# Fused attention, soft-MoE and squared-ReLU FFN on one core: the second layer's first pass cut into a quarter and a half of the inner dimension, with two weight slots moved behind w2

## The chip, the cores and the metric

The kernel runs on one NeuronCore of a Trainium2 chip. The metric is the device time of one execution in microseconds (us). The core has a matrix engine (PE, with its weight loads listed apart as PEld), a vector engine (DVE), a scalar engine (ACT), a general engine (POOL), and a queue engine (SP) that issues every DMA of this kernel, in program order.

## The reference, cut to what matters

Three layers follow one another. The last two concern us here.

```python
# attention in chunks of 32 rows, 4 x 8 heads, gives x: 3072 x 512
logits = x @ phi                              # 3072 x 32
slot_input = softmax(logits, axis=0).T @ x    # 32 x 512
for e in range(8):                            # 4 slots per expert
    slot_out[e] = relu(slot_input[e] @ w1[e]) @ w2[e]    # 512 -> 1024 -> 512
x = softmax(logits, axis=1) @ slot_out        # c @ slot_out, 3072 x 512
h = x @ w_in                                  # 512 -> 2048
g = s * relu(h) ** 2 + b
out = g @ w_out                               # 2048 -> 512
```

w1 and w2 are 16 MB each and are read once. w_in and w_out come as float64, 8 MB each, and are read as pairs of 32-bit words; the kernel turns each 1 MB piece into float32 with shifts, masks and multiplications.

## The kernel before, in words

**First part.** Attention and the sums over tokens run until about 126 us. Meanwhile SP loads w1 into sixteen slots of SBUF, 1 MB each.

**Slot stage.** `emit_w1` (8 steps) and `emit_w2` (16 steps) compute slot_out, 32 rows at a time, with weights as the moving operand. The slots of w1 are refilled with w2 as they come free, by `load_w`, which issues the next entries of the list `order`. Before the change `order` holds two pieces of w_in (numbers 2 and 3, the list `EARLY`) ahead of the last four pieces of w2. Between the steps of `emit_w2` PE transposes the gate c into `cpack` (`pack_c`), and at steps 11 and 12 it does two bursts of four matmuls whose product nobody reads (`warm(4)`, the fillers).

**Second layer.** h is not computed from x: since x = c @ slot_out, the kernel forms M = slot_out @ w_in (32 rows, kept in `mpack`) and then h = c @ M. The inner dimension of 2048 is cut into 16 columns of 128, called f, and into four groups of four f, called fb. M is made one fb at a time: `m_part` for fb 0, and `emit_m` and `emit_m2` for fb 1 to 3, at the items listed in `M_AT`.

**Items.** The work of the second layer is a list of 112 items, each one block of tokens and one f. Four blocks of 384 tokens (A: two, B: two) go in pairs, and three blocks of 512 tokens (C) go singly. For item n PE makes h (`emit_h`); ACT does relu, square and the rounded high part `ghi`; DVE makes the low part `glo`; and PE, three items later (`LA`), adds three products per 128 tokens into PSUM: ghi and glo with the high part `w_hi` of w_out (`emit_o`), ghi with the low part `w_lo` (`emit_o2`). At the end of a block's run the sums leave PSUM: whole ones go to the output, half ones wait in `part`. With `HF` = 8 the runs are: A over f 0 to 7, B over all 16, C over all 16, A over f 8 to 15.

**Conversions.** The table `cq` says at which item k a piece of w_in ("i", fb, j) or w_out ("o", f) is converted: one ACT operation (`cv_act`, line 579), three DVE operations (lines 589, 591, 598), and for w_out one more on ACT (line 813) and two more on DVE (lines 806, 808). Before the change they come every second item, from item 0 to 46. The w_in pieces of fb 0 and of fb 1 are converted in the slot stage instead (`early`, eight `tasks`). The 1 MB pieces pass through three slots in turn (`NRG`); `load_w` fills one when the conversion that read it last is done.

**What sets the order.** Each engine takes its instructions in the order in which the code emits them: `for n in range(LA + 1, ...)` at the end is the loop over items. There is no planner.

Of the kernel before, what the change touches and what calls it, by code (L numbers as in the profile page):

```python
# [26 lines left out]
SLOT = 2048  # L27
# [7 lines left out]
def kernel(  # L35
# [81 lines left out]
    with tc.manual_schedule():  # L117
# [45 lines left out]
        NRG, E_AT = 3, 4  # L163
        EARLY = [("wi", 2), ("wi", 3)]
# [26 lines left out]
        def load_w(n, cap=None):  # L191
            for _ in range(n):
                i = wnext[0]
                if i < (len(order) if cap is None else cap):
                    src = srcs[order[i][0]][order[i][1]]
                    p = at_[order[i]] if i < npre else (16 + (i - npre) % NRG) * SLOT
# [385 lines left out]
        def cv_dve(key, j):  # L582
            h, lf, a, w = cv[key]
            hi, ai = h.bitcast(I32), a.bitcast(I32)
            if key[0] == "i" and key[1] > 1:
# [104 lines left out]
        tasks = [("i", j // 4, j % 4) for j in range(8)]  # L690

        def early(k, part):
            key = tasks[k]
            if part == 0:
                cv_act(key, 0 if k < 4 else k % 2, wi_src(*key[1:]))
                cv_dve(key, 0)
            else:
                cv_dve(key, 2)
                cv_low(key, cv[key][1].rearrange("p (k f) -> p k f", k=2))
                wi_add(key)  # L700

        for i in range(9):
            if i < 8:
                emit_w1(i)
                if i >= 1:
                    load_w(2, npre - E_AT - len(EARLY))
                if i == 0:
# [59 lines left out]
        wide_r, wide_r2 = at512(18 * SLOT, 2), at512(18 * SLOT + 1024, 2)  # L767
# [5 lines left out]
        HF = NF // 2  # L773
# [3 lines left out]
        runs = [[(x, 0, HF) for x in A], [(x, 0, NF) for x in B]]  # L777
        runs += [[(x, 0, NF)] for x in C] + [[(x, HF, NF)] for x in A]
# [6 lines left out]
        part = [tiles("part", 3, DM), [area(19 * SLOT + DM * t, DM) for t in range(NTU)]]  # L785
        h_t, o_t = {}, {}

        def stage_a(k):
            key = cq.get(k)
            if key:  # L790
                if key[0] == "i":
                    w = wi_src(key[1], key[2])
                else:
                    w = wt[raw_of[key]].rearrange("p (f d t) -> p f d t", f=2, t=2)[:, key[1] % 2]
                cv_act(key, k // 2 % 2, w)
# [19 lines left out]
        def emit_m(fb):  # L815
            wis = wis_b if fb % 2 else wis_a
            mp = psum("s", [128, 512])
            for lo in range(1 if fb == 1 else 2):
                for kc in range(KD):
                    lhsT, rhs = (soTb[:, kc, :], wis_l[:, kc, :]) if lo else (soT4[:, kc, 0, :], wis[kc // 2][:, kc % 2, :])  # L820
                    nc.tensor.matmul(out=mp[32 * kc:32 * kc + 32, :], lhsT=lhsT, rhs=rhs,
                                     start=(lo == 0), stop=(lo == 1 or fb == 1))
# [24 lines left out]
        def emit_hs(n):  # L847
            if n < len(items):
                if wide(n) or n // 2 - 1 in (M_AT[1] // 2, M_AT[2] // 2):
# [35 lines left out]
        wsum_hl = [cpack[:, 128 * B[0][0] + DM * x:128 * B[0][0] + DM * (x + 1)] for x in range(2)]  # L885
# [15 lines left out]
        def os_early(j, t):  # L901
            return area(16 * SLOT + DM * (NTU * j + t), DM)

        def add_bias(i):
            j, t = divmod(i, NTU)
            os_ = os_early(j, t) if j < 2 else part[j - 2][t]
            nc.gpsimd.tensor_tensor(out=os_, in0=os_, in1=bias, op=ALU.add)  # L907
            if j < 2:
                store(B[j][0] + t, os_)
# [17 lines left out]
        def emit_o2(n):  # L927
# [3 lines left out]
            for t in range(nt):  # L931
# [5 lines left out]
                if f == f1 - 1:  # L937
                    if r_[0] in B or f1 == HF:
                        to = os_early(B.index(r_[0]), t) if r_[0] in B else part[A.index(r_[0])][t]
                        if t == 1:  # L940
                            nc.scalar.activation(out=to, in_=o, func=AF.Copy, scale=sbt[:, 0:1])
                        else:
                            nc.vector.tensor_scalar(out=to, in0=o, scalar1=sbt[:, 0:1], scalar2=None, op0=ALU.mult)
                    else:
                        os_ = os_g[t]
                        nc.vector.scalar_tensor_tensor(out=os_, in0=o, scalar=sbt[:, 0:1],
                                                       in1=part[A.index(r_[0])][t] if f0 else bias,
# [75 lines left out]
        for n in range(LA + 1, len(items) + LA + 1):  # L1023
# [7 lines left out]
            if n == 2 * HF + 3:  # L1031
# [20 lines left out]
            if n != 2 * HF + 2:  # L1052
                convert(n)
            if 48 <= n < 64:
# [8 lines left out]
            while n != 2 * HF + 2 and wnext[0] < len(order) and last_use.get(order[wnext[0] - NRG], -1) <= n:  # L1063
# [73 lines left out]
```

## Time and profile before

| | us |
|---|---|
| median of 3 runs (lowest, highest) | 470.21 (468.28, 471.7) |
| profiled execution, its own time | 470.53 |
| its span, first to last instruction | 468.7 |
| PE busy in the span | 448.5 (96%) |
| ACT, DVE, POOL busy | 298.0, 285.5, 85.2 |
| mean granted clock of PE | 0.999 of full speed |

The time outside the span is 1.8 us. All 40 slices of the span show the granted clock at 9 tenths or more. The mean DMA rate is about 400 GB/s until 164 us, and then falls, because the weights are in. How to read it: a row of the timeline gives start and duration, then engine, line, operation and tiles; in brackets stands how long the engine had been idle and what ended that. Durations of neighbouring matmuls overlap, so the step from one start to the next is the cost of one, not the duration.

### The profile page before, as it was taken

Reading aid. Unit: us, or ns where it says so; the run is one execution under the profiler, and the core shown is the slowest. Engines: PE = TensorE matmul, PEld = TensorE weight load, DVE = VectorE, ACT = ScalarE, POOL = GpSimd, SP = SyncE. Lnnn points to the kernel's source line nnn. Section 1 sums busy time; section 2 is a strip of 40 time slices with the busy share of each in tenths; the row PEclk is TensorE's granted clock in tenths of the full one; section 3 lists DMA queues with packets and bytes.
Section 4 is the critical chain, followed back from the end, with each engine's and each line's share of the span. In section 5 each row is a group of like instructions: output and inputs, shape, how many; then the busy total and the mean of one; then the engine's idle time right before and its main releaser. Section 6 shows DMA issues by size and latency. Waiting matters only on the chain.

```text
span 468.7 us, 10048 instructions
## 1 busy us (share of the span) xinstructions
PE 448.5 (96%) x3936; PEld 339.6 (72%) x3936; DVE 285.5 (61%) x637; ACT 298.0 (64%) x588; POOL 85.2 (18%) x154
## 2 busy tenths in 40 slices
PE   6879999999899989999999999999999999999996
PEld 5656666666545556888786887888888888888885
DVE  5768888877466659978284988765642242224242
ACT  4556666657234559978686988666666666665670
POOL 6655556562000000000000000000690000000000
PEclk9999999999999999999999999999999999999999
DMA  8999999998999963424232000000320020002011
GB/s 298 357 398 385 404 407 405 405 403 324 402 418 421 415 280 96 175 89 162 89 109 90 0 2 0 1 0 1 123 103 1 0 89 2 0 2 87 2 69 67
DMA packets 20575, 83.03 MB, mean 177 GB/s; under 512 B 2736, under 2 KB 2864, under 8 KB 14640
## 3 DMA queue, kind: packets, MB, share of 16 engines
q1 hardware_dynamic: 20528, 82.39, 45.5%
q8 instruction: 31, 0.51, 0.4%
q14 instruction: 16, 0.13, 0.1%
HBM read 76.09 MB, written 6.29 MB: 176 GB/s over the span
## 4 chain that ended last, share of the span: by engine, by line
PE 71%; DMA 15%; DVE 6%; ACT 4%; issue 1%; SPq 1%; POOL 1%; DVEq 0%; POOLq 0%; ACTq 0%
PE g L924 12%; DMA vals<-in_vm_dram 6%; PE lp L924 6%; PE pt L924 6%; PE xt L924 6%; PE x L924 6%; PE g L936 6%; PE s L843 4%; DMA keys<-in_w_out_dram 4%; DMA seg<-in_w_dram 3%; PE s L285 3%; PE xt L936 3%; PE pt L936 3%; PE lp L936 3%; PE x L936 3%; PE x L325 3%
## 5 line engine op out<-in xcount | busy, mean ns | idle before, releaser
L878 DVE TENSOR_TENSOR glo<-vals,ghi 128x512 fp32r<-128x512 f32 x48 | 35.9, 752 | 63.2 <-ACT ghi L874 63.2
L866 ACT ACTIVATE vals<-s 128x512 f32<-128x512 f32 x48 | 28.7, 597 | 45.3 <-PE s L843 45.3
L878 DVE TENSOR_TENSOR glo<-r,ghi 128x384 fp32r<-128x384 f32 x64 | 35.4, 555 | 19.7 <-ACT ghi L874 19.5
L866 ACT ACTIVATE r<-s 128x384 f32<-128x384 f32 x64 | 31.2, 487 | 16.6 <-PE s L843 16.6
L301 ACT ACTIVATE seg<-seg 128x384 f32<-128x384 f32 x32 | 28.8, 899 | 19.8 <-DVE seg L312 15.6
L907 POOL TENSOR_TENSOR keys<-keys,bias 128x512 f32<-128x512 f32 x6 | 8.8, 1493 | 173.4 <-ACT vals L866 173.4
L936 PE MATMUL g<-wlo,ghi 128*128 128x512 f32 x128 | 39.6, 389 | 0.0
L924 PE MATMUL g<-whi,ghi 128*128 128x512 f32 x126 | 39.3, 390 | 0.0
L924 PE MATMUL g<-whi,glo 128*128 128x512 f32 x126 | 39.1, 389 | 0.0
L843 PE MATMUL s<-cpack,mpack 128*128 128x384 f32 (+1 forms) x112 | 36.9, 368 | 0.5 <-ACT r L866 0.4
L870 ACT ACTIVATE r<-r 128x384 f32<-128x384 f32 x64 | 33.6, 526 | 4.7 <-DVE glo L878 2.8
L263 POOL TENSOR_SCALAR keys<-keys 64x416 f32<-64x416 f32 x63 | 33.7, 534 | 13.9 <-PE lp L346 3.1
L285 PE MATMUL s<-keys 128*32 128x128 f32 x768 | 30.3, 291 | 4.6 <-POOL keys L267 3.3
L874 ACT CAST ghi<-r 128x384 fp32r<-128x384 f32 x64 | 32.6, 509 | 1.7 <-PE g L936 0.4
L325 PE MATMUL x<-vals,seg 128*32 128x128 f32 x744 | 27.8, 275 | 5.3 <-DMA vals<-in_vm_dram 4.4
L870 ACT ACTIVATE vals<-vals 128x512 f32<-128x512 f32 x48 | 30.4, 634 | 1.8 <-DVE glo L878 0.2
L325 PEld LDWEIGHTS x<-vals,seg 128*32 128x32 f32 x744 | 20.5, 109 | 15.0 <-DVE seg L309 5.2
L874 ACT CAST ghi<-vals 128x512 fp32r<-128x512 f32 x48 | 29.8, 621 | 1.5
L936 PEld LDWEIGHTS g<-wlo,ghi 128*128 128x128 f32 x128 | 24.0, 188 | 5.0
L924 PEld LDWEIGHTS g<-whi,glo 128*128 128x128 f32 x126 | 23.7, 188 | 5.1
L285 PEld LDWEIGHTS s<-keys 128*32 128x32 f32 x768 | 19.5, 113 | 10.6 <-POOL keys L267 6.0
L924 PEld LDWEIGHTS g<-whi,ghi 128*128 128x128 f32 x126 | 23.7, 188 | 4.5 <-issue 0.2
(257 smaller groups left out, 1052.3 us busy)
## 6 DMA issues: line engine op xcount, KB each, us to landing
seg<-in_w_dram SPq DMA_DIRECT2D x27, 1024.0 KB, 8.8
keys<-in_kq_dram SPq DMA_DIRECT2D x32, 396.0 KB, 7.4
vals<-in_vm_dram SPq DMA_DIRECT2D x64, 192.0 KB, 6.7
keys<-in_w_in_dram SPq DMA_DIRECT2D x5, 1024.0 KB, 5.0
keys<-in_w_out_dram SPq DMA_DIRECT2D x5, 1024.0 KB, 4.8
out_dram<-seg SPq DMA_DIRECT2D x18, 256.0 KB, 2.1
vals<-in_w_in_dram SPq DMA_DIRECT2D x3, 1024.0 KB, 8.6
vals<-in_w_out_dram SPq DMA_DIRECT2D x3, 1024.0 KB, 4.8
```

The lines of the kernel that those rows point to most:

```text
L263: (nc.vector if h and u == 0 else nc.gpsimd).tensor_scalar(out=stream(kz[rows, h], 0, CH), in0=k[rows, UT * h:UT * h + (NCU + 1) * CH].rea ...
L285: nc.tensor.matmul(out=o, lhsT=qt[:, 32 * c:32 * c + 32], rhs=kz[:, :, at:at + WIN], start=True, stop=not (first or last))
L301: nc.scalar.activation(out=p_r[u], in_=sm_r[u].rearrange("p t h (a r) -> p t r (h a)", a=2), func=AF.Exp, scale=scale)
L325: nc.tensor.matmul(out=xp[32 * r:32 * r + 32, t], lhsT=pts_r[u][:, 32 * c:32 * c + 32], rhs=vbuf[u // 2 % 2][:, u % 2, :, 64 * c:64 * c + ...
L843: nc.tensor.matmul(out=hq, lhsT=mpack[:, 128 * f:128 * f + 128], rhs=cpack[:, 128 * t0:128 * (t0 + nt)], start=True, stop=True)
L866: nc.scalar.activation(out=r_of(n), in_=h_t.pop(n), func=AF.Relu)
L870: nc.scalar.activation(out=r2_of(n), in_=r_of(n), func=AF.Square)
L874: nc.scalar.copy(out=g_of(n)[0], in_=r2_of(n))
L878: nc.vector.tensor_tensor(out=glo, in0=r2_of(n), in1=ghi.bitcast(F32), op=ALU.subtract)
L907: nc.gpsimd.tensor_tensor(out=os_, in0=os_, in1=bias, op=ALU.add)
L924: nc.tensor.matmul(out=o_t[r_][t], lhsT=g[x][:, 128 * t:128 * t + 128], rhs=w_hi[f], start=(first and x == 0), stop=False)
L936: nc.tensor.matmul(out=o, lhsT=ghi[:, 128 * t:128 * t + 128], rhs=w_lo[f], start=False, stop=(f == f1 - 1))
```

## The change

The items are cut differently: A runs over f 0 to 3 (`HA`), then B over f 0 to 7 (`HB`), then A over f 4 to 15, then C, then B over f 8 to 15. There are again 112 items. The order of the conversions changes with it: w_out f 0 to 3 at items 0, 2, 4, 6; w_in fb 1 at 7, 8, 9, 11; w_out f 4 to 7 at 13, 15, 17, 19; w_in fb 2 at 21 to 24 and fb 3 at 27 to 30; the rest of w_out as before. `early` keeps the four pieces of fb 0 only. The two pieces of w_in of fb 1 leave their place ahead of w2's last four pieces; they are loaded after w_out 0 and 1. The pieces pass through two slots instead of three. The sum for fb 1 moves from item 4 to item 12, and has a low part now, as those for fb 2 and 3 have. The fillers in the slot stage are gone. w2's last piece comes in three DMAs instead of two. Partial sums wait in other places, and half sums are added to in one more place on DVE and twice on POOL (`add_part`).

```diff
-        NRG, E_AT = 3, 4
-        EARLY = [("wi", 2), ("wi", 3)]
         order = [("w1", i) for i in range(W1)] + [("wi", 0), ("wi", 1)] + [("w2", i) for i in range(W2)]
...
-        order = order[0:-E_AT] + EARLY + order[-E_AT:]
-        order[W1:W1 + 3] = [("w2", 0), ("wi", 0), ("wi", 1)]
         npre = len(order)
-        at_.update({key: (18 + i) * SLOT for i, key in enumerate(EARLY)})
-        cq = {}
-        for j in range(8):
-            cq[2 * j] = ("o", j)
-            cq[16 + 2 * j] = ("i", 2 + j // 4, j % 4)
-            cq[32 + 2 * j] = ("o", 8 + j)
+        cq = {32 + 2 * j: ("o", 8 + j) for j in range(8)}
+        cq.update({k: ("o", j) for j, k in enumerate((0, 2, 4, 6, 13, 15, 17, 19))})
+        for fb, ks in enumerate(((7, 8, 9, 11), (21, 22, 23, 24), (27, 28, 29, 30))):
+            cq.update({k: ("i", fb + 1, j) for j, k in enumerate(ks)})
+        cbuf = {k: n % 2 for n, k in enumerate(sorted(cq))}
...
+        for n in range(npre, len(order)):
+            at_[order[n]] = (18 if n == npre + 2 else 16 + (n - npre - (n > npre + 2)) % 2) * SLOT
+        gate = {order[n]: max((last_use[key] for key in order[npre:n] if at_[key] == at_[order[n]]), default=-1)
+                for n in range(npre, len(order))}
...
-                        for x in range(2):
-                            nc.sync.dma_start(out=wt[order[i]][x], in_=src[:, SLOT // 2 * x:SLOT // 2 * (x + 1)])
+                        for x, w in ((0, 2), (2, 1), (3, 1)):
+                            at = slice(SLOT // 4 * x, SLOT // 4 * (x + w))
+                            nc.sync.dma_start(out=t[:, at], in_=src[:, at])
...
-        tasks = [("i", j // 4, j % 4) for j in range(8)]
+        tasks = [("i", 0, j) for j in range(4)]
...
                 if i >= 1:
-                    load_w(2, npre - E_AT - len(EARLY))
+                    load_w(2, npre)
...
-            if i == 2:
-                load_w(len(EARLY) + E_AT)
-            if i == 10:
-                load_w(2)
-            if i == 14:
-                load_w(1)
-            if i in (11, 12):
-                warm(4)
+            if i == 0:
+                load_w(3)
...
-            if 7 <= i < 15:
-                early(4 + (i - 7) // 2, (i - 7) % 2)
...
-        M_AT = (4, 26, 34)
+        M_AT = (12, 26, 34)
...
-        HF = NF // 2
+        HA, HB = NF // 4, NF // 2
...
-        runs = [[(x, 0, HF) for x in A], [(x, 0, NF) for x in B]]
-        runs += [[(x, 0, NF)] for x in C] + [[(x, HF, NF)] for x in A]
+        runs = [[(x, 0, HA) for x in A], [(x, 0, HB) for x in B], [(x, HA, NF) for x in A]]
+        runs += [[(x, 0, NF)] for x in C] + [[(x, HB, NF)] for x in B]
+        TURN = (2 * HA, 2 * HA + 2 * HB)
...
-            for lo in range(1 if fb == 1 else 2):
+            for lo in range(2):
...
+        def add_part(j):
+            nc.gpsimd.tensor_tensor(out=os_early(j, 1), in0=os_early(j, 1), in1=part[j][1], op=ALU.add)
...
+                        elif f1 < NF:
+                            nc.vector.tensor_scalar(out=to, in0=o, scalar1=sbt[:, 0:1], scalar2=None, op0=ALU.mult)
                         else:
-                            nc.vector.tensor_scalar(out=to, in0=o, scalar1=sbt[:, 0:1], scalar2=None, op0=ALU.mult)
+                            nc.vector.scalar_tensor_tensor(out=to, in0=o, scalar=sbt[:, 0:1], in1=part[x][t],
+                                                           op0=ALU.mult, op1=ALU.add)
...
-            late = m + 1 < len(items) and m + 1 == 2 * HF + 1
+            late = m in TURN
...
-            if n != 2 * HF + 2:
+            if n - 2 not in TURN:
                 convert(n)
+            if n in (53, 55):
+                add_part((n - 53) // 2)
...
-            while n != 2 * HF + 2 and wnext[0] < len(order) and last_use.get(order[wnext[0] - NRG], -1) <= n:
+            while n - 2 not in TURN and wnext[0] < len(order) and gate[order[wnext[0]]] <= n:
                 load_w(1)
```

On the SP queue, at the end of the slot stage's loads (`w_dram` is w1 or w2, `seg` 93 to 96 the slots of w2's last four pieces):

```order
-L212 DMA vals_103<-in_w_in_dram 128x2048
-L212 DMA vals_104<-in_w_in_dram 128x2048
 L212 DMA seg_93<-in_w_dram 128x2048
 L212 DMA seg_94<-in_w_dram 128x2048
 L212 DMA seg_95<-in_w_dram 128x2048
-L207 DMA seg_96<-in_w_dram 128x1024 x2
+L207 DMA seg_96<-in_w_dram 128x1024
+L207 DMA seg_96<-in_w_dram 128x512 x2
 L212 DMA keys<-in_w_out_dram 128x2048 x2
```

Two loads of 1 MB no longer stand ahead of w2's last four pieces and of w_out's first two.

On ACT, from the square of item 3 to the square of item 5, before the change (`ghi` is the high part of g, `whi` that of w_out, `mps` and `mpack` belong to the sum of M for fb 1):

```order
L870 ACTIVATE r_2650<-r_2648 128x384
L874 CAST ghi_2654<-r_2650 128x384
L579 ACTIVATE seg_99<-keys 128x512
L823 COPY mps_2646<-s 128x512
L866 ACTIVATE r_2647<-s 128x384
L870 ACTIVATE r_2649<-r_2647 128x384
L874 CAST ghi_2655<-r_2649 128x384
L813 CAST whi_2616<-seg_99 128x512
L832 CAST mpack<-s 128x512
L866 ACTIVATE r_2648<-s 128x384
L870 ACTIVATE r_2650<-r_2648 128x384
```

The same stretch after it:

```order
L864 ACTIVATE r_2619<-r_2617 128x384
L868 CAST ghi_2623<-r_2619 128x384
L579 ACTIVATE seg_99<-keys 128x512
L860 ACTIVATE r_2616<-s 128x384
L864 ACTIVATE r_2618<-r_2616 128x384
L868 CAST ghi_2624<-r_2618 128x384
L807 CAST whi_2585<-seg_99 128x512
L860 ACTIVATE r_2617<-s 128x384
L864 ACTIVATE r_2619<-r_2617 128x384
```

The copy `mps` and the cast into `mpack` have left this place; they stand at items 12 and 13 now.

On DVE, from item 9 to item 11 of the changed kernel, where the first run of A ends (line 941 takes sums out of PSUM into `part`; line 598 ends the conversion of a w_in piece into `seg_101`):

```order
L591 TENSOR_SCALAR seg_99<-vals_103 128x512
L598 SCALAR_TENSOR_TENSOR seg_101<-keys,seg_99 128x2x256
L941 TENSOR_SCALAR vals_103<-pt,cstt 128x512
L941 TENSOR_SCALAR vals_103<-xt,cstt 128x512
L872 TENSOR_TENSOR glo_2629<-r_2619,ghi_2624 128x384
L941 TENSOR_SCALAR vals_103<-lp,cstt 128x512
L941 TENSOR_SCALAR vals_104<-g,cstt 128x512
L589 TENSOR_SCALAR vals_104<-keys 128x2x256
L872 TENSOR_TENSOR glo_2625<-r_2618,ghi_2620 128x384
L591 TENSOR_SCALAR keys<-vals_104 128x512
L598 SCALAR_TENSOR_TENSOR seg_101<-keys 128x2x256
```

The last row here ends the conversion that the moved sum of M for fb 1 reads; four sums out of PSUM stand between it and the conversion before.

## Rows read from the trace of the kernel before

**Rows 1.** The windows view: busy time (instructions) by engine, clock, DMA share, GB/s.

```profile
159.50:166.90 7.40, 7.40 (x90) 4.17 (x86) 5.41 (x10) 1.91 (x5) 0.00 (x0) 1.00 1.01 415
166.90:171.90 5.00, 3.05 (x21) 2.05 (x17) 1.74 (x6) 2.98 (x8) 0.00 (x0) 1.00 0.93 382
171.90:186.40 14.50, 13.93 (x60) 9.64 (x61) 13.38 (x27) 14.08 (x30) 0.00 (x0) 1.00 0.22 84
186.40:208.00 21.60, 21.60 (x98) 18.08 (x98) 19.26 (x37) 20.05 (x42) 0.00 (x0) 1.00 0.43 148
```

**Rows 2.** The chain of waits: start us, us, what ended last.

```profile
135.48 15.73 DMA seg<-in_w_dram
...
151.28 18.33 DMA keys<-in_w_out_dram
```

**Rows 3.** Timeline of PE, 159 to 187 us: start us, us, operation, [idle before].

```profile
159.49 0.61 PE L449 MATMUL lp<-ident 128*128 128x256 bf16 x4
160.03 1.07 PE L666 MATMUL xt<-seg,seg 128*32 128x256 f32 x16
...
161.31 0.60 PE L449 MATMUL lp<-ident 128*128 128x256 bf16 x4
161.84 1.07 PE L666 MATMUL xt<-seg,seg 128*32 128x256 f32 x16
...
169.63 0.62 PE L843 MATMUL s<-cpack,mpack 128*128 128x384 f32 x2
...
186.14 0.44 PE L843 MATMUL s<-cpack,mpack 128*128 128x384 f32 x1 [0.40 <-ACT r L866]
```

**Rows 4.** Timeline of ACT, 168 to 188 us.

```profile
168.99 0.27 ACT L832 CAST mpack<-pt 128x128 fp32r<-128x128 f32 x1 [0.80 <-PE pt L686]
169.70 0.66 ACT L579 ACTIVATE seg<-keys 128x512 f32<-128x512 f32 x1 [0.45 <-DMA keys<-in_w_out_dram]
170.27 0.48 ACT L866 ACTIVATE r<-s 128x384 f32<-128x384 f32 x1
...
178.52 0.59 ACT L823 COPY mps<-s 128x512 f32<-128x512 f32 x1
179.00 0.50 ACT L866 ACTIVATE r<-s 128x384 f32<-128x384 f32 x1
...
180.51 0.62 ACT L813 CAST whi<-seg 128x512 fp32r<-128x512 f32 x1
181.10 0.59 ACT L832 CAST mpack<-s 128x512 fp32r<-128x512 f32 x1
181.58 0.50 ACT L866 ACTIVATE r<-s 128x384 f32<-128x384 f32 x1
...
185.60 0.49 ACT L866 ACTIVATE r<-s 128x384 f32<-128x384 f32 x1
...
187.52 0.48 ACT L866 ACTIVATE r<-s 128x384 f32<-128x384 f32 x1
```

**Rows 5.** Timeline of PE, h matmuls around the sum of M at 228 us.

```profile
217.19 0.51 PE L843 MATMUL s<-cpack,mpack 128*128 128x384 f32 x2
...
226.08 0.51 PE L843 MATMUL s<-cpack,mpack 128*128 128x384 f32 x2
...
237.31 0.51 PE L843 MATMUL s<-cpack,mpack 128*128 128x384 f32 x2
```

**Rows 6.** Timeline of DVE at the turn between two runs.

```profile
211.80 0.74 DVE L943 TENSOR_SCALAR vals<-g,cstt 128x512 f32<-128x512 f32 x1
212.46 0.42 DVE L591 TENSOR_SCALAR keys<-seg 128x512 int32<-128x512 int32 x1
212.91 0.69 DVE L598 SCALAR_TENSOR_TENSOR seg<-keys 128x512 bf16<-128x512 uint32 x1
213.51 0.55 DVE L878 TENSOR_TENSOR glo<-r,ghi 128x384 fp32r<-128x384 f32 x1
```

**Rows 7.** Page, section 6: a DMA issue, KB, us from issue to landing.

```profile
keys<-in_w_in_dram SPq DMA_DIRECT2D x5, 1024.0 KB, 5.0
```

More of the change, by code (lines that the diff above doesn't have):

```diff
@@ L195, in load_w @@
                     src = srcs[order[i][0]][order[i][1]]
-                    p = at_[order[i]] if i < npre else (16 + (i - npre) % NRG) * SLOT
+                    p = at_[order[i]]
                     if p is SPLIT:
@@ L584, in cv_dve @@
             hi, ai = h.bitcast(I32), a.bitcast(I32)
-            if key[0] == "i" and key[1] > 1:
+            if key[0] == "i" and key[1] > 0:
                 ai = wi_dst(wis_b if key[1] % 2 else wis_a, key).bitcast(I32)
@@ L694, in early @@
             if part == 0:
-                cv_act(key, 0 if k < 4 else k % 2, wi_src(*key[1:]))
+                cv_act(key, 0, wi_src(*key[1:]))
                 cv_dve(key, 0)
@@ L765, in at512 @@
             return [area(pos + 512 * i, 512) for i in range(n)]
-        wide_r, wide_r2 = at512(18 * SLOT, 2), at512(18 * SLOT + 1024, 2)
+        wide_r, wide_r2 = at512(17 * SLOT, 2), at512(17 * SLOT + 1024, 2)
         os_g = at512(13 * SLOT, 4)
@@ L784 @@
             items += [(r_, f) for f in range(rs[0][1], rs[0][2]) for r_ in rs]
-        part = [tiles("part", 3, DM), [area(19 * SLOT + DM * t, DM) for t in range(NTU)]]
+        part = [at512(18 * SLOT, 3), [area(18 * SLOT + 3 * DM, DM), bias, area(19 * SLOT + 3 * DM, DM)]]
+        part += [tiles("part", 3, DM), at512(19 * SLOT, 3)]
         h_t, o_t = {}, {}
@@ L794, in stage_a @@
                     w = wt[raw_of[key]].rearrange("p (f d t) -> p f d t", f=2, t=2)[:, key[1] % 2]
-                cv_act(key, k // 2 % 2, w)
+                cv_act(key, cbuf[k], w)
         def stage_d(k, j):
@@ L821, in emit_m @@
                     nc.tensor.matmul(out=mp[32 * kc:32 * kc + 32, :], lhsT=lhsT, rhs=rhs,
-                                     start=(lo == 0), stop=(lo == 1 or fb == 1))
+                                     start=(lo == 0), stop=(lo == 1))
             nc.scalar.copy(out=mps, in_=mp)
@@ L848, in emit_hs @@
             if n < len(items):
-                if wide(n) or n // 2 - 1 in (M_AT[1] // 2, M_AT[2] // 2):
+                if wide(n) or n // 2 - 1 in [x // 2 for x in M_AT]:
                     emit_h(n)
@@ L883, in wsum_add @@
                 nc.vector.tensor_tensor(out=wsum, in0=a, in1=(w_hi, w_lo)[i % 2][i // 2].bitcast(F32), op=ALU.add)
-        wsum_hl = [cpack[:, 128 * B[0][0] + DM * x:128 * B[0][0] + DM * (x + 1)] for x in range(2)]
+        wsum_hl = [cpack[:, 128 * t:128 * t + DM] for t in (A[0][0], C[0][0])]
         def wsum_split():
@@ L901, in os_early @@
         def os_early(j, t):
-            return area(16 * SLOT + DM * (NTU * j + t), DM)
+            return area(16 * SLOT + DM * j, DM) if t == 1 else part[j][t]
+        def add_part(j):
+            nc.gpsimd.tensor_tensor(out=os_early(j, 1), in0=os_early(j, 1), in1=part[j][1], op=ALU.add)
         def add_bias(i):
             j, t = divmod(i, NTU)
-            os_ = os_early(j, t) if j < 2 else part[j - 2][t]
+            os_ = os_early(j, t) if j < 2 else part[j][t]
             nc.gpsimd.tensor_tensor(out=os_, in0=os_, in1=bias, op=ALU.add)
             if j < 2:
-                store(B[j][0] + t, os_)
+                store(A[j][0] + t, os_)
         def emit_o(n, parts=(0, 1)):
@@ L937, in emit_o2 @@
                 if f == f1 - 1:
-                    if r_[0] in B or f1 == HF:
-                        to = os_early(B.index(r_[0]), t) if r_[0] in B else part[A.index(r_[0])][t]
+                    x = (A + B).index(r_[0]) if r_[0] in A + B else None
+                    if f1 < NF or x in (0, 1):
+                        to = part[x][t] if f1 < NF else os_early(x, t)
                         if t == 1:
                             nc.scalar.activation(out=to, in_=o, func=AF.Copy, scale=sbt[:, 0:1])
-                        else:
-                            nc.vector.tensor_scalar(out=to, in0=o, scalar1=sbt[:, 0:1], scalar2=None, op0=ALU.mult)
+                        elif f1 < NF:
+                            nc.vector.tensor_scalar(out=to, in0=o, scalar1=sbt[:, 0:1], scalar2=None, op0=ALU.mult)
+                        else:
+                            nc.vector.scalar_tensor_tensor(out=to, in0=o, scalar=sbt[:, 0:1], in1=part[x][t],
+                                                           op0=ALU.mult, op1=ALU.add)
                     else:
@@ L946, in emit_o2 @@
                         nc.vector.scalar_tensor_tensor(out=os_, in0=o, scalar=sbt[:, 0:1],
-                                                       in1=part[A.index(r_[0])][t] if f0 else bias,
+                                                       in1=bias if x is None else part[x][t],
                                                        op0=ALU.mult, op1=ALU.add)
@@ L1027 @@
             ends = 0 <= m and items[m][1] == items[m][0][2] - 1
-            late = m + 1 < len(items) and m + 1 == 2 * HF + 1
+            late = m in TURN
             if ends or late:
                 emit_o2(m)
-            if n == 2 * HF + 3:
+            if n - 3 in TURN:
                 convert(n - 1)
```

## The prediction, made before the changed kernel was run

> **What bounds the kernel now.** Read the windows view first, for the stretch that the change touches. At the end of the slot stage, 159.5 to 166.9 us, PE is busy 7.40 of 7.40 us while the DMA share is 1.01 at 415 GB/s [rows 1]: both are full, so one must ask which of them the other would wait for. PE's own rows answer: its steps follow one another without a bracket, and the fillers stand among them [rows 3]. So PE does not wait for w2 there. The transfers end only just in time: the chain of waits goes through two DMAs, the second of them w_out's first piece, which is issued at 151.28 and lands at 169.6 [rows 2], and ACT's first conversion had idled 0.45 us for it [rows 4]. From 166.9 to 171.9 PE is busy 3.05 of 5.00 us [rows 1]; there it follows copies and casts. From 186.4 to 208 it is busy 21.60 of 21.60 [rows 1], and no view shows it idle again until the tail. From about 186 us on, then, whatever PE must do more is paid in full, and only what shortens PE's work or moves its start is gained.
>
> The stretch between, 171.9 to 186.4, decides the sign. PE's busy time is 13.93 of 14.50 us, which reads as full. But it holds 60 matmuls, one in 0.242 us, where the next window has 98 in 21.60, one in 0.220; and PEld is busy 9.64 of 14.50 us (66%) against 18.08 of 21.60 (84%) [rows 1]. At its end the ninth h matmul waits 0.40 us for ACT's relu of item 7 [rows 3]. So this stretch, the ramp, goes at ACT's pace. The Trainium skill, page Trainium Kernel Development and Optimization, section Best Practices, says that matmul busy time is a bad measure of TensorE because matmuls are pipelined, and that the share of LDWEIGHTS is a better one. By that rule the ramp is not full, which the two shares above bear out; by busy time it is full, and the sum would be that of the first rival.
>
> **The change part by part.**
>
> *Fillers.* Two bursts of four matmuls cost PE 160.03 - 159.49 = 0.54 and 161.84 - 161.31 = 0.53 us [rows 3]. They lie on PE's path, which nothing interrupts: -1.07 us. The cover that could be missing is w2's data; it comes earlier now, as the next step says.
>
> *Two loads behind w2.* 2 x 1.05 MB at 415 GB/s [rows 1] are 5.0 us. So w2's last pieces and w_out 0 land 5 us earlier. PE gets none of that for w2, since it did not wait. What it gets is the 0.45 us at w_out 0: ACT was free at 168.99 + 0.27 = 169.26, and could start the conversion then and not at 169.70 [rows 4]. The relu behind it needs the first h matmul, though, one of a pair that runs from 169.63 to 170.25 [rows 3]; I estimate its product at 170.0. So relu moves from 170.27 to about 170.0: -0.25. Together with the fillers the second layer starts 1.3 us earlier. w_in 2 and 3 now land behind w_out; they are not needed before items 7 and 9, some 12 us after the layer starts, against 5.0 us for one such load [rows 7]: nothing.
>
> *The ramp on ACT.* The sum for fb 1 leaves it: the copy `mps` from 178.52 to the relu at 179.00, 0.48 us, and the cast into `mpack` from 181.10 to the relu at 181.58, 0.48 us [rows 4]. The conversion of w_in at item 7 is new in it. An item with one such conversion and no `whi` takes 187.52 - 185.60 = 1.92 us from relu to relu; without it, the way from relu at 179.00 to the end of `ghi` at 180.51 is 1.51 [rows 4]; so +0.41. By item 7's relu ACT is ahead by 1.3 + 0.48 + 0.48 - 0.41 = 1.85 us; I take 1.8, because DVE's steps between gain only the 1.3. The ninth h matmul, which waits for it, comes at 184.3 and not at 186.14 [rows 3]. From there PE is full, as before.
>
> *The sum of M for fb 1.* Before, its PE work lay in the ramp, where PE had room, and so cost nothing. Now it stands at item 12, behind the ramp, and has a low part like the others. Its price there is that of the sum for fb 2 at 228 us: four items without a sum go from the h pair at 217.19 to that at 226.08, 8.89 us; the next four, with it, to 237.31, 11.23 us [rows 5]. The difference, 2.34 us, is paid in full: +2.3.
>
> *The first turn.* A's run ends at item 7 now, among dense conversions. DVE steps there cost 0.66 us for a sum out of PSUM (211.80 to 212.46), 0.45 for line 591, 0.60 for line 598 and 0.47 for `glo` [rows 6]; with 0.4 for line 589 a conversion of w_in is 1.45. For items 7 to 11 that makes 4 x 1.45 + 4 x 0.66 + 5 x 0.47 + 1.4 for the rest of w_out 3, in all 12.2 us, against five items of PE at 8.89 / 4 = 2.22 us, or 11.1. DVE falls about 1.1 us behind. The moved sum needs the last conversion of these, at item 11, one item later. PE uses `glo` about two items after it is made, which hides most of it. Ends: nothing (the old turn, in the window to 208 us and beyond, shows no idle of PE) and 2.6 us (all four sums out of PSUM in PE's way). I take +0.4, near the end that a row shows.
>
> *The rest, at nothing.* The second turn, at item 24, has the same six sums as the old one, and conversions before and behind it rather than in it; if they collided it would be the first turn's 0.4 again. Two slots instead of three: a piece is asked for after the last use of its slot and is needed four to five items later, 8.9 us or more at PE's pace, against 5.0 us to land [rows 7]; for the tightest, w_in 5, ACT runs ahead by an item or two, and PE would feel it only when ACT's lead is gone. The two adds on POOL and the third DMA of w2's last piece are issued by queues that nothing waits for there. h matmuls and products are as many as before.
>
> **The sum.** -1.8 (which holds the 1.07 and the 0.25) + 2.34 + 0.4 = +0.94 us. The profiled execution took 470.53 us, 0.3 above the median of 470.21, and would take 471.5; from the median it is 471.2, which I forecast: no change that can be measured.
>
> **The rivals.**
>
> *The ramp is PE's, as its busy time says.* Then moving the sum of M is moving PE work within PE's path, and costs only its new low part: four matmuls side by side in the array's columns, by estimate the time of one product, 0.23 us (2.22 us hold nine and an h). The start's 1.3 us are kept. 470.21 - 1.3 + 0.23 + 0.4 gives 469.5. For it: 13.93 of 14.50. Against it: 0.242 us per matmul, and ACT's relu as the last releaser. 20%.
>
> *The slot stage goes at the DMA's pace.* If the fillers only filled waits, the second layer starts as much earlier as w_out 0 lands: -5.0 and not -1.3. Then 470.21 - 5.0 + 2.34 + 0.4 = 467.9. For it: the DMA share of 1.01, and w_out 0 in the chain. Against it: the products of the slot stage stand at even steps of PE, with and without a filler between. 7%.
>
> *DVE chokes at the first turn.* The place is between items 9 and 12. If the sums out of PSUM wait behind whole conversions, PE waits for its banks, and then for the conversion of item 11, without which M for fb 1 and so h for f 4 cannot come. It decides from the point where line 598 of item 11 ends later than PE's products of item 12. Price: the 2.6 us above in place of the 0.4: 473.4, slower than before; with a collision at the second turn too, 475.6. For it: 12.2 us of work in 11.1. Against it: two items' lead. 15%, a quarter of it with both turns.
>
> *PE's clock falls.* The granted clock is 1.00 in all four windows, also where PE idles 1.95 of 5.00 us [rows 1]; this is the higher of its levels, 2.4 GHz. The Trainium skill, page TensorE: Matmul & The Clock Gate, section The HAM clock gate, says that a PE left idle drops to half its clock, which speaks against taking fillers out. If it happened, the slot stage's end would take its 7.4 us of PE work again: 470.21 + 0.94 + 7.4 = 478.6. The trace disagrees so far as it goes, since the longer idle stretch keeps 1.00, and the change leaves no new gap. 2%.
>
> That the loads do not move is excluded by the order of the SP queue.
>
> **The numbers.** 56% for the forecast, with a range of its own from 470.0 to 472.5. With 20, 7, 15 and 2% for the others, the range that leaves out no more than two in ten goes from 468.4 (the sum of M free, -1.8) to 474.1 (-1.07 for the fillers alone, 2.34 and 2.6). The bound of what a measurement of this kernel can tell is 1%, 4.7 us. Faster than 465.5 needs more than the second rival gives: 3%. Slower than 474.9 takes both turns or the clock: 6%. Within: 91%.
>
> **What would show it.** In the changed profile the fillers' rows are gone and PE still has no bracket from 144 to 166 us; ACT's first conversion has no wait for a DMA; the first product with w_out 0 starts at about 170.6; the ninth h matmul at about 184.3; a step of 11.2 us and not 8.9 over the four items around item 12; no PE idle of more than 0.5 us at the first turn. I am wrong if the ninth h matmul comes before 183 (the first rival), if the slot stage ends before 164.5 (the second), or if PE waits for DVE at line 941 or 598 (the third).

## The result, and the profile after

| | before | changed |
|---|---|---|
| median of 15 runs each (lowest, highest), us | 469.39 (468.19, 471.7) | 472.79 (470.56, 473.79) |
| ratio to before, 95% interval | | 1.007 [1.0056, 1.0084] |
| profiled execution: its time, span, mean granted clock | 470.53, 468.7, 0.999 | 473.79, 472.0, 0.989 |

The changed kernel is 0.7% slower: 3.3 us by the ratio (2.6 to 3.9), where +0.94 was forecast. It lies in the range and inside 1%, but more than two thirds of the difference come from a place at which the prediction had entered nothing.

First the steps that came as foretold. In this execution the part ahead of the slot stage is 1.17 us shorter than in that of before. Executions of one kernel differ there by more (2.26 us in the second experiment, whose first part is that of before), so this isn't put down to the change. The first matmul of w1 shows it, of before and then of the changed kernel:

```profile
125.92 3.66 PE L628 MATMUL s<-seg,keys 128*32 128x256 f32 x64
```

```profile
124.75 3.66 PE L628 MATMUL s<-seg,keys 128*32 128x256 f32 x64
```

Every comparison below of a start with one of before takes these 1.17 us out. PE at the end of the slot stage, to be held against [rows 3]: at the two places where the fillers stood, the steps of w2 follow without a bracket, and there is no line 449 among them any more.

```profile
157.31 1.07 PE L666 MATMUL pt<-seg,seg 128*32 128x256 f32 x16
158.20 1.05 PE L666 MATMUL xt<-seg,seg 128*32 128x256 f32 x16
159.17 0.44 PE L677 MATMUL g<-ident,seg 128*128 128x128 f32 x2
159.54 1.07 PE L666 MATMUL xt<-seg,seg 128*32 128x256 f32 x16
```

ACT's start into the second layer, against [rows 4]: the conversion at line 579 has no bracket for a DMA.

```profile
166.85 0.68 ACT L579 ACTIVATE seg<-keys 128x512 f32<-128x512 f32 x1
```

Then PE: the first product, in before and then in the changed kernel, the h matmul that the prediction calls the ninth (that of item 9, if one counts from 0), and the h matmuls around the sum of M at item 12, which now lies on a full PE, as that of [rows 5] does.

```profile
171.89 0.50 PE L924 MATMUL pt<-whi,ghi 128*128 128x512 f32 x1 [1.21 <-ACT ghi L874]
```

```profile
169.45 0.50 PE L921 MATMUL pt<-whi,ghi 128*128 128x512 f32 x1 [1.07 <-ACT ghi L868]
...
183.24 0.45 PE L837 MATMUL s<-cpack,mpack 128*128 128x384 f32 x1 [1.72 <-ACT r L860]
187.62 0.51 PE L837 MATMUL s<-cpack,mpack 128*128 128x384 f32 x2
192.26 0.51 PE L837 MATMUL s<-cpack,mpack 128*128 128x384 f32 x2
...
203.49 0.51 PE L837 MATMUL s<-cpack,mpack 128*128 128x384 f32 x2
```

The four items from 192.26 to 203.49 take 11.23 us, the same number as in [rows 5]. At the h pair of 203.49 the account of the first part can be closed, since before had that pair at 203.85:

```profile
203.85 0.51 PE L843 MATMUL s<-cpack,mpack 128*128 128x384 f32 x2
```

203.49 + 1.17 - 203.85 = +0.81 us, where the sum of the prediction gave +0.94. So what the prediction worked out is there by 204 us, and right within 0.13 us. The other 2.5 us must come later. The list of PE's waits names the place: "PE lp L921 <- DVE vals L943: 1.9", a wait that before has not. It is at the border between A's second run and C's, 285 to 296 us. DVE and POOL there:

```profile
285.01 0.75 DVE L943 SCALAR_TENSOR_TENSOR vals<-pt,cstt,vals 128x512 f32<-128x512 f32 x1 [0.79 <-PE pt L933]
285.68 0.74 DVE L943 SCALAR_TENSOR_TENSOR vals<-xt,cstt,vals 128x512 f32<-128x512 f32 x1
286.34 1.52 DVE L872 TENSOR_TENSOR glo<-keys,ghi 128x512 fp32r<-128x512 f32 x1
287.78 0.68 DVE L877 TENSOR_TENSOR wsum<-wsum,whi 128x512 f32<-128x512 f32 x1
288.49 1.73 DVE L877 TENSOR_TENSOR wsum<-wsum,wlo 128x512 f32<-128x512 f32 x1
290.15 0.74 DVE L943 SCALAR_TENSOR_TENSOR vals<-lp,cstt,vals 128x512 f32<-128x512 f32 x1
```

```profile
286.01 1.30 POOL L899 TENSOR_TENSOR keys<-keys,vals 128x512 f32<-128x512 f32 x1 [128.18 <-ACT keys L939]
288.40 1.28 POOL L899 TENSOR_TENSOR keys<-keys,bias 128x512 f32<-128x512 f32 x1 [1.09 <-ACT keys L939]
```

The same stretch of DVE before:

```profile
285.20 0.75 DVE L943 TENSOR_SCALAR keys<-pt,cstt 128x512 f32<-128x512 f32 x1 [0.80 <-PE pt L936]
...
286.53 0.68 DVE L878 TENSOR_TENSOR glo<-vals,ghi 128x512 fp32r<-128x512 f32 x1
...
287.85 0.69 DVE L883 TENSOR_TENSOR wsum<-wsum,wlo 128x512 f32<-128x512 f32 x1
288.46 0.74 DVE L943 TENSOR_SCALAR keys<-lp,cstt 128x512 f32<-128x512 f32 x1
```

Each of POOL's two adds (`add_part`, new) lies over one DVE operation with two inputs in SBUF, and that one takes 1.52 and 1.73 us in place of 0.68 and 0.69. The sum of `xt`, which has one input in PSUM, runs beside POOL from 286.01 to 286.34 and keeps its 0.74. DVE takes its work in the order of its queue, so the sum of `lp` starts at 290.15, 5.14 us behind that of `pt`; before it is 288.46 - 285.20 = 3.26. PE needs that PSUM bank at once, and has no slack there: in before, the sum ends at 288.46 + 0.74 = 289.20, and PE's first product into the bank starts at 289.25. So the 1.88 us more on DVE become 1.89 us of idle time on PE. PE before, and then changed:

```profile
289.25 0.50 PE L924 MATMUL lp<-whi,ghi 128*128 128x512 f32 x1
```

```profile
290.94 0.50 PE L921 MATMUL lp<-whi,ghi 128*128 128x512 f32 x1 [1.89 <-DVE vals L943]
...
291.51 0.60 PE L837 MATMUL s<-cpack,mpack 128*128 128x512 f32 x1
...
295.15 0.39 PE L933 MATMUL pt<-wlo,ghi 128*128 128x512 f32 x1
```

Behind the idle time there is a second loss. The nine steps from the h matmul at 291.51 to the first product with `w_lo` at 295.15 take 3.64 us, 0.40 each, with durations of 0.6 and not 0.39 us. The windows view (busy us by engine, then granted clock, DMA share, GB/s) gives a clock of 0.66 there, a mean of the two levels, 1.2 and 2.4 GHz; in the 5 us ahead of it and behind it the clock is 1.00. (Most of what takes the mean clock of this execution to 0.989 is elsewhere, in the first part: 0.82 from 5 to 10 us and 0.50 from 10 to 15.)

```profile
290.00:295.00 5.00, 4.06 (x11) 3.24 (x12) 4.93 (x9) 1.97 (x4) 0.00 (x0) 0.66 0.00 0
```

At the higher level the same nine steps take 2.05 us (the first experiment has them), so this loss is 1.6 us. In sum 0.81 + 1.89 + 1.6 = 4.3 us against 473.79 + 1.17 - 470.53 = 4.43 us between the two profiled executions; the last 0.1 us are not followed here.

### The profile page after: what moved, and what is told of

Its sections match the earlier page's. It is cut to its first block, busy times and chain, and to the rows that moved or that the text cites. A ratio compares the mean times of both kernels' runs of the same rounds, so it can differ in the third digit from the quotient of the medians.

```text
span 472.0 us, 10051 instructions
## 1 busy us (share of the span) xinstructions
PE 449.9 (95%) x3932; PEld 340.2 (72%) x3932; DVE 285.5 (60%) x637; ACT 298.8 (63%) x590; POOL 87.5 (19%) x156
## 4 chain that ended last, share of the span: by engine, by line
PE 75%; DVE 8%; DMA 7%; ACT 4%; POOL 2%; SPq 1%; issue 1%; DVEq 0%; POOLq 0%; ACTq 0%
PE g L921 11%; DMA vals<-in_vm_dram 6%; PE pt L921 6%; PE lp L921 6%; PE xt L921 6%; PE x L921 6%; PE g L933 6%; PE s L837 4%; PE s L628 3%; PE pt L933 3%; PE lp L933 3%; PE xt L933 3%; PE x L933 3%; PE x L325 3%; PE s L285 2%; PE xt L666 2%
## 5 line engine op out<-in xcount | busy, mean ns | idle before, releaser
L872 DVE TENSOR_TENSOR glo<-keys,ghi 128x512 fp32r<-128x512 f32 x48 | 36.9, 774 | 64.5 <-ACT ghi L868 64.5
L860 ACT ACTIVATE keys<-s 128x512 f32<-128x512 f32 x48 | 28.7, 598 | 48.7 <-PE s L837 48.7
L837 PE MATMUL s<-cpack,mpack 128*128 128x384 f32 (+1 forms) x112 | 37.9, 375 | 1.8 <-ACT r L860 1.7
L921 PE MATMUL g<-whi,ghi 128*128 128x512 f32 x126 | 39.3, 391 | 0.0
L921 PE MATMUL g<-whi,glo 128*128 128x512 f32 x126 | 39.2, 390 | 0.0
L864 ACT ACTIVATE keys<-keys 128x512 f32<-128x512 f32 x48 | 30.3, 632 | 1.8 <-DVE glo L872 0.3
L868 ACT CAST ghi<-keys 128x512 fp32r<-128x512 f32 x48 | 29.9, 622 | 1.5
L921 PEld LDWEIGHTS g<-whi,glo 128*128 128x128 f32 x126 | 23.7, 188 | 5.0
L319 ACT COPY seg<-pt 128x384 f32<-128x384 f32 x32 | 15.2, 475 | 19.0 <-PE pt L317 18.1
L921 PE MATMUL lp<-whi,ghi 128*128 128x512 f32 x63 | 25.2, 399 | 1.9 <-DVE vals L943 1.9
```

The source lines that it names most:

```text
L319: nc.scalar.copy(out=pts_r[u], in_=pt)
L837: nc.tensor.matmul(out=hq, lhsT=mpack[:, 128 * f:128 * f + 128], rhs=cpack[:, 128 * t0:128 * (t0 + nt)], start=True, stop=True)
L860: nc.scalar.activation(out=r_of(n), in_=h_t.pop(n), func=AF.Relu)
L864: nc.scalar.activation(out=r2_of(n), in_=r_of(n), func=AF.Square)
L868: nc.scalar.copy(out=g_of(n)[0], in_=r2_of(n))
L872: nc.vector.tensor_tensor(out=glo, in0=r2_of(n), in1=ghi.bitcast(F32), op=ALU.subtract)
```

## The experiments

The theory after this reading: POOL's adds slow DVE at the border, PE idles for it, and PE's clock falls behind that. The rival: the terms of the prediction are simply larger than worked out, and the idle time is harmless or has another cause. The medians of one group of runs are held against runs of before on the same chip, whose medians there were 468.9 to 469.0.

**The adds issued later.**

```diff
-            if n in (53, 55):
-                add_part((n - 53) // 2)
+            if n in (58, 61):
+                add_part((n - 58) // 3)
```

> The changed kernel with one edit: POOL's two adds of A's parts (line 899) are issued at items 58 and 61 instead of 53 and 55, so that they no longer run beside DVE's sums out of PSUM and its `glo` at the end of A's second run. Theory (the adds slow DVE there, PE idles 1.9 us for the sum of `lp`, and its clock falls behind that idle time): no PE idle over 0.3 us between 285 and 296 us, `glo` and the `wsum` add at about 0.7 us each, the clock back at 1.00, and the time 2 to 3.7 us below the changed kernel's 472.8: 469.1 to 470.8. Rival (the sum of M on a full PE and the first turn are the whole loss): 472.8 within 0.5, whatever DVE does at the border.

Measured: 472.51 us, ratio 1.0076 [1.0053, 1.0099], as the changed kernel. But the theory isn't hit by it, for the edit did not do what it said. POOL at the border, and PE behind it:

```profile
285.70 1.30 POOL L899 TENSOR_TENSOR keys<-keys,vals 128x512 f32<-128x512 f32 x1 [128.16 <-ACT keys L939]
```

```profile
290.64 0.50 PE L921 MATMUL lp<-whi,ghi 128*128 128x512 f32 x1 [1.89 <-DVE vals L943]
...
291.21 0.39 PE L837 MATMUL s<-cpack,mpack 128*128 128x512 f32 x1
...
293.26 0.39 PE L933 MATMUL pt<-wlo,ghi 128*128 128x512 f32 x1
```

POOL had nothing else in its queue for 128 us. A place further down the program holds an instruction back only by what stands ahead of it on its own engine; here nothing does, so the add still starts when ACT has written its input. What the run does tell: the same idle time of 1.89 us, and in this execution the nine steps behind it take 2.05 us, at a clock of 1.00. So the idle time and the fall of the clock are two losses, and the second does not follow in every execution. This one took 471.98 us, that of the changed kernel 473.79. The 15 runs of the changed kernel lie in two groups, seven from 470.56 to 472.13 and eight from 472.79 to 473.79; that the clock parts them is shown for the two executions with a profile, for the others it is only likely. The mean clock of each run fits it (0.986 to 0.993 in the eight, 0.993 to 1.000 in the seven), but doesn't settle it, because that mean holds the first part too.

**The adds alone, in the kernel before.**

```diff
+            if n in (53, 55):
+                add_dummy((n - 53) // 2)
```

`add_dummy` is POOL's add with the inputs os_early(j, 1) and part[j][1], written to os_g[j].

> The kernel before with one addition: two POOL adds of the same shape at the same items, 53 and 55, whose result goes to two areas that are overwritten later. It makes more work than the kernel before, nothing that the output needs. Theory: DVE's `glo` and `wsum` adds at the border between B's run and C's take 1.5 to 1.7 us in place of 0.7, PE idles 1 to 2 us for a sum out of PSUM, and the time is 470.4 to 473.1 against 469.4. Rival (POOL disturbs nobody): 469.4 within 0.5.

Measured: 470.95 us, ratio 1.0042 [1.0024, 1.0061], 2.0 us slower (1.1 to 2.9). DVE, and PE:

```profile
285.60 1.51 DVE L878 TENSOR_TENSOR glo<-vals,ghi 128x512 fp32r<-128x512 f32 x1
...
287.75 1.74 DVE L883 TENSOR_TENSOR wsum<-wsum,wlo 128x512 f32<-128x512 f32 x1
```

```profile
290.20 0.50 PE L927 MATMUL lp<-whi,ghi 128*128 128x512 f32 x1 [1.89 <-DVE keys L946]
```

Two instructions of 1.3 us on an engine that nobody waits for cost 2.0 us, and nothing else of the change is in this kernel. The rival falls. One more row of this execution bears on the second rival of the prediction:

```profile
160.63 1.07 PE L666 MATMUL xt<-seg,seg 128*32 128x256 f32 x16 [0.39 <-DMA seg<-in_w_dram]
```

The part ahead of the slot stage was 2.26 us shorter here than in the first profile of before, and then PE does wait for w2, here and once more for 0.34 us. So the kernel before stands close to the DMA's pace at the end of the slot stage: in this execution its loads, not its PE, cost it some 0.7 us there, in the first profile nothing.

**DVE's queue freed at the border.** The `wsum` adds are DVE work there that can wait.

```diff
-            if 48 <= n < 64:
-                for i in (2 * n - 96, 2 * n - 95):
+            if 53 <= n < 64:
+                for i in range(3 * n - 159, min(3 * n - 156, 32)):
```

> The changed kernel with DVE's `wsum` adds kept off the border between A's second run and C's: none at items 48 to 52, three and not two per item from 53 on. POOL's two adds stay where they ran. Theory (PE's 1.89 us come from DVE reaching the sum of `lp` late; its queue there holds a `wsum` add of 1.74 us beside POOL's): the sum of `lp` starts 2.4 to 3 us earlier, PE's idle time is under 0.3 us, the clock does not fall behind it, and the time is 469.3 to 471.2. Rival (POOL's add alone, by the 1.5 us `glo`, is enough to hold PE): 1 us or more of idle time stays and the time is above 471.5.

Measured: 469.44 us, ratio 1.0012 [0.9996, 1.0028]. DVE, then the window:

```profile
285.28 1.51 DVE L872 TENSOR_TENSOR glo<-keys,ghi 128x512 fp32r<-128x512 f32 x1
286.72 0.74 DVE L943 SCALAR_TENSOR_TENSOR vals<-lp,cstt,vals 128x512 f32<-128x512 f32 x1
```

```profile
285.00:300.00 15.00, 15.00 (x68) 12.43 (x67) 12.63 (x18) 11.26 (x19) 2.55 (x2) 1.00 0.00 0
```

`glo` is as slow as before beside POOL, but the sum of `lp` comes right behind it, PE is busy 15.00 of 15.00 us and the clock stays. What remains, +0.56 us (-0.2 to +1.3), is the prediction's own sum, 0.94 forecast and 0.81 read from rows.

**The adds held back by data.** A copy that reads the `ghi` of item 58 or 61 stands ahead of each add in POOL's queue.

```diff
-            if n in (53, 55):
-                add_part((n - 53) // 2)
+            if n in (58, 61):
+                nc.gpsimd.tensor_copy(out=gpad[:, 0:64], in_=g_of(n)[0][:, 0:64].bitcast(F32))
+                add_part((n - 58) // 3)
```

> The changed kernel with POOL's two adds held back by data: ahead of each a copy of 64 columns reads the `ghi` of item 58 and 61, so that POOL cannot start it at 286 us. Theory: the adds run near 312 to 325 us beside a DVE that is idle half the time, no PE idle over 0.3 us between 285 and 296 us, `glo` there 0.7 us, clock 1.00 in that window, and the time as in the run with the moved `wsum` adds, 469.3 to 471.2. Rival (the idle time has another cause than POOL): 472.5 within 0.5.

Measured: 470.05 us, ratio 1.0021 [1.0006, 1.0036]. POOL, and DVE at the border:

```profile
310.77 1.75 POOL L899 TENSOR_TENSOR keys<-keys,vals 128x512 f32<-128x512 f32 x1
```

```profile
286.62 0.68 DVE L872 TENSOR_TENSOR glo<-keys,ghi 128x512 fp32r<-128x512 f32 x1
```

Now the adds are where the first experiment had wished them; `glo` is back at 0.68, and PE has no wait for DVE, though the add at 310.77 again lies beside a `wsum` add that takes 1.68 us: there PE needs nothing of DVE at once. Its +1.0 us (0.3 to 1.7) agrees with the run before it. Of the changed kernel's 3.3 us some 2.3 to 2.7 hang on these two adds, the fall of the clock included.

**The sum of M twice.** The price of the term that the prediction thought the largest.

```diff
-        M_AT = (12, 26, 34)
+        M_FB = {12: 1, 26: 2, 34: 3, 36: 3}
```

> The changed kernel with the sum of M for fb 3 made twice (at items 34 and 36), the same values both times. It prices one sum of M at a place where PE is full. Theory, by the prediction's term: +2.3 us over the changed kernel, 475.1. Rival (the sum's matmuls lie side by side and cost little): at most +0.5, 473.3.

Measured: 474.64 us, ratio 1.0121 [1.0096, 1.0146], some 2.1 us above the changed kernel and its copy in the first experiment. In rows, from the single h matmul behind the sum at 34 to the h pair three pairs on; the changed kernel, then this one:

```profile
252.37 0.74 PE L837 MATMUL s<-cpack,mpack 128*128 128x384 f32 x1
...
266.49 0.51 PE L837 MATMUL s<-cpack,mpack 128*128 128x384 f32 x2
```

```profile
253.68 0.74 PE L837 MATMUL s<-cpack,mpack 128*128 128x384 f32 x1
...
270.07 0.51 PE L837 MATMUL s<-cpack,mpack 128*128 128x384 f32 x2
```

16.39 - 14.12 = 2.27 us for one sum on a full PE; the term was 2.34.

**The fillers put back.**

```diff
+            if i in (11, 12):
+                warm(4)
```

> The changed kernel with the two bursts of fillers put back at steps 11 and 12 of the slot stage. Theory, by the prediction's term: +1.07 us, 473.9, and a first product 1.07 us later. Rival (the removed fillers let PE's clock fall): the clock is back at 1.00 and the time at 472 or less.

Measured: 473.81 us, ratio 1.0088 [1.0066, 1.011], against 1.0076 for the copy of the changed kernel on the same chip, which alone would not decide it. The rows do:

```profile
123.95 3.66 PE L628 MATMUL s<-seg,keys 128*32 128x256 f32 x64
...
169.78 0.50 PE L923 MATMUL pt<-whi,ghi 128*128 128x512 f32 x1 [1.07 <-ACT ghi L870]
```

From the first matmul of w1 to the first product 45.83 us, against 169.45 - 124.75 = 44.70: +1.13, with 1.07 forecast. The clock's fall has nothing to do with them: PE has the wait of 1.9 us for DVE here too, and the clock of 285 to 300 us is 0.89 as in the changed kernel.

**An attempt at a faster version: ACT relieved in the ramp.** It starts from the kernel with the moved `wsum` adds, and casts `whi` of items 2, 4 and 6 on POOL.

```diff
+                if k in (2, 4, 6):
+                    nc.gpsimd.tensor_copy(out=w_hi[key[1]], in_=cv[key][2])
+                else:
```

> The run with the moved `wsum` adds, and the cast into `whi` of items 2, 4 and 6 on POOL, which idles there, and no longer on ACT. Theory (the ramp goes at ACT's pace; each cast holds ACT 0.52 us): ACT is 1.56 us ahead at item 7's relu, PE's wait of 1.7 us ahead of the ninth h matmul shrinks to under 0.5 us, and the time is 1.2 to 1.6 us below the run with the moved `wsum` adds. Rival (POOL's cast is slower and disturbs DVE, so that DVE's conversions become the bound): the wait stays over 1 us or turns into one for DVE, no gain.

Measured: 469.95 us, ratio 1.0016 [0.9998, 1.0034]: no gain. PE:

```profile
170.96 0.50 PE L924 MATMUL pt<-whi,ghi 128*128 128x512 f32 x1 [1.07 <-ACT ghi L871]
...
183.53 0.44 PE L840 MATMUL s<-cpack,mpack 128*128 128x384 f32 x1 [0.41 <-ACT r L863]
...
192.59 0.50 PE L924 MATMUL pt<-whi,ghi 128*128 128x512 f32 x1 [1.14 <-DVE vals L944]
```

The ramp did get shorter: from the first product to the ninth h matmul 12.57 us and not 13.79, so the ramp goes at ACT's pace, as the prediction said. But the 1.2 us are given back at the first turn, where PE now waits 1.14 us for DVE's sum of `pt`, which stands behind two conversions in its queue. That is the rival of this run, and POOL is in it once more. One of its casts, and two of DVE's operations beside a cast:

```profile
182.80 1.01 POOL L808 CAST whi<-keys 128x512 fp32r<-128x512 f32 x1 [2.74 <-DVE keys L589]
```

```profile
179.61 0.99 DVE L598 SCALAR_TENSOR_TENSOR seg<-keys,seg 128x512 f32<-128x512 uint32 x1
...
183.25 0.83 DVE L591 TENSOR_SCALAR keys<-keys 128x512 int32<-128x512 int32 x1
```

Beside the three casts line 591 takes 0.83 us twice, where it takes 0.42 elsewhere, and line 598 takes 0.99 and not 0.69. That is 1.1 us in all, and DVE is never idle between these operations and the sum of `pt`. By this estimate the casts make nearly the whole wait of 1.14 us. How late DVE would be at the turn with a shorter ramp and no work on POOL, no run here shows.

**ACT takes two of the three sums at the first turn.**

```diff
-                        if t == 1:
+                        if t == 1 or t == 0 and f1 == HA:
```

> The run with `whi` on POOL and, at the first turn, two of each block's three sums out of PSUM on ACT (the first as well as the second), one on DVE. Theory (the 1.2 us that the ramp gained were given back at the first turn, where DVE is late with the sum of `pt`): PE's wait of 1.1 us for DVE there shrinks to under 0.6 us, the time falls by 0.8 to 1.7 us, to 468.2 to 469.2, which is 0 to 0.7 us below the kernel before. Rival (ACT is as full there, and its relu comes later by as much): no gain, 470 within 0.5.

The casts stay on POOL here and in the next run. Measured: 470.2 us, ratio 1.0031 [1.0018, 1.0043]: no gain. The waits at the turn are now two, 0.69 us for DVE and 0.68 for ACT:

```profile
190.37 0.50 PE L924 MATMUL xt<-whi,ghi 128*128 128x512 f32 x1 [0.69 <-DVE vals L944]
...
192.42 0.45 PE L840 MATMUL s<-cpack,mpack 128*128 128x384 f32 x1 [0.68 <-ACT r L863]
```

**One conversion moved by an item.**

```diff
-            for fb, ks in enumerate(((7, 8, 9, 11), (21, 22, 23, 24), (27, 28, 29, 30))):
+            for fb, ks in enumerate(((7, 8, 10, 11), (21, 22, 23, 24), (27, 28, 29, 30))):
```

> As the run with two sums on ACT, and the third w_in conversion of fb 1 one item later (items 7, 8, 10, 11 in place of 7, 8, 9, 11), so that none is made at the item in which the sums out of PSUM begin. Theory (DVE reaches the sums behind two conversions): a further 0 to 0.6 us, 467.8 to 469.2. Rival (the sum of M at item 12 needs the conversions, and they are later now): PE waits for line 598 ahead of the sum of M, and the time is 0.3 us or more above the run without this edit.

Measured: 470.64 us, ratio 1.0034 [1.0021, 1.0046]. DVE's wait is gone, and ACT's has grown to 1.84 us:

```profile
192.96 0.44 PE L840 MATMUL s<-cpack,mpack 128*128 128x384 f32 x1 [1.84 <-ACT r L863]
```

In these two executions the waits add up to 1.84 us against 0.69 + 0.68; the medians, 470.64 and 470.2, are too close to tell the runs apart. The rival's mechanism isn't there in any case: PE waits for a relu, not for line 598. Between items 7 and 13, with the casts on POOL, what is taken from DVE comes back on ACT. No version here beats the kernel before; the one with the moved `wsum` adds can't be told from it.

## Why the prediction was right, and which step of it failed

- *Fillers, the two loads, the start of the second layer:* -1.3 us forecast; 169.45 + 1.17 - 171.89 = -1.27. The fillers' 1.07 came back as 1.13 when they were put back, which leaves 0.14 for the two loads, where 0.25 was forecast. ACT's wait for w_out is gone, as said. Right.
- *The ramp on ACT:* the ninth h matmul 1.8 us earlier; 183.24 + 1.17 - 186.14 = -1.73. That PE waits 1.72 us for ACT there, and that relieving ACT moves it, excludes the first rival.
- *The sum of M:* +2.34 forecast, 2.34 by the step of four items (11.23 and 8.89), 2.27 when doubled. Right.
- *The first turn:* +0.4 forecast. The step over it, 187.62 to 192.26, is 4.64 us, where a pair elsewhere takes 8.89 / 2 = 4.45: +0.2, with no wait of PE for DVE. Near the lower end, as chosen. PE did wait for DVE at this turn when the ramp was 1.2 us shorter, but with POOL's casts beside DVE; that the third rival was nearer than its 15% said is not shown.
- *The rest, at nothing: "The two adds on POOL and the third DMA of w2's last piece are issued by queues that nothing waits for there."* This is the step that failed. It is true that nobody waits for POOL. But the sentence asks only who waits for the engine's result, and not whom the engine holds up while it works. The adds doubled two DVE operations at the one place where DVE's queue ends in a sum that PE needs at once. Their price, 1.89 us of idle time, and 1.6 us of low clock in executions where it falls, is larger than the whole forecast. The trace of before held the price: POOL's `add_bias`, from 332 us on, runs beside `glo`, which takes 4.18 us for three in place of 0.7 each. PE does not wait for it there (it is busy 13.00 of 13.00 us from 332 to 345), so no wait pointed at it.

```profile
337.83 4.18 DVE L878 TENSOR_TENSOR glo<-vals,ghi 128x512 fp32r<-128x512 f32 x3
```

- *The fourth rival, the clock:* the fall came, but not where the rival put it and not by the fillers. The prediction's "the change leaves no new gap" is wrong with the step above. The stretch that it leant on (PE idle 1.95 of 5.00 us at clock 1.00, [rows 1]) holds its idle time in several pieces, the longest 1.21 us in before's trace; in the changed kernel a piece of 1.72 us ahead of the h matmul at 183.24 keeps 1.00 as well. The one of 1.89 us at the border stands in five profiled executions: the lower level follows in three (the changed kernel, the sum of M twice, the fillers put back) and not in two (the adds issued later, the adds alone in before). The six profiled executions without it show no fall there. The length of a wait alone does not decide it: in its first part, at 28.19 us, before's trace has one of 2.58 us for a DMA, and the clock stays at 1.00.

The Trainium skill, page SBUF — State Buffer, section Who interferes with whom, says that a VectorE instruction with two SBUF inputs contends with a GpSimd instruction that reads SBUF, that one with at most one SBUF input, outside the modes in which VectorE takes two ports, does not, and that the ports the two engines share are an exclusive lock, so that the later of the two blocks until the other is done. The traces agree on all three: `glo` and the `wsum` add (two inputs in SBUF) go from 0.68 and 0.69 to 1.52 and 1.73 us, the sum of `xt` (one in PSUM) stays at 0.74, and `glo`, issued at 286.34 while POOL works until 287.31, ends at 287.86, 0.55 us later, not quite the 0.68 of a whole `glo`, as the `wsum` add of 288.49 ends 0.54 us behind POOL's second add. By that sentence the adds could have been priced ahead, as an estimate: two blocked operations of up to 1.3 us each, at a border where the trace of before shows no slack.

The median moved by 3.4 us and was forecast to move by 0.94 because the parts with a wait to follow were right and the part without one was not looked into. The forecast's own range, 470.0 to 472.5, does not hold the 472.79. That the time stayed in the wider range is luck: its upper end was made for other mishaps.

## What to carry to other kernels

An engine that nobody waits for is not free: ask, at the very microsecond at which its work will run, which other engine shares its way into SBUF, and what that one owes to the bottleneck next. And that microsecond is set by data, not by the line: on an idle queue an instruction runs as soon as its inputs are there, so a delay must be a dependence. Where a helper engine must work at a border, keep deferrable work of its neighbour (here `wsum`) away from the border; that bought back 2.7 of 3.3 us with two changed lines.

## What the runs showed of the hardware that was not expected

- A POOL add of 128x512 float32 that takes 1.30 us stretches a DVE operation with two SBUF inputs from 0.68 to 1.51 us, or from 0.69 to 1.74; held back, POOL's own add takes 1.75 us, behind a `wsum` add that started 0.14 us before it.
- POOL's cast, which has one input, disturbs DVE's one-input integer steps as well: beside a cast of 1.01 us line 591 takes 0.83 and not 0.42 us.
- The same idle time of 1.89 us on PE was followed by some 3 us at the lower clock in three profiled executions and by none in two others.
